# The opening's gated outputs, h and w_down's parts move from pools of their own into the buffers of the later rounds

## The chip, the core and the metric

The kernel runs on one core of a Trainium2 chip. Its engines are TensorE (PE, with weight loads shown apart as PEld), VectorE (DVE), ScalarE (ACT), GpSimd (POOL, hardly used here) and SyncE (SP, which issues nearly all DMAs). Each engine takes the instructions of its own queue strictly in the order in which they stand there, and waits on semaphores for the others. The metric is the device time of one launch in microseconds (us): 1403.15 us is the median of 3 runs before the change (1402.41 to 1403.16).

## The reference

Cut to what matters, with x of 2048 rows by 576 columns, w_gate and w_up of 576 by 4608 and w_down of 4608 by 576:

```python
def _A_ref(x, w_r, w_i):
    X = rfft2(x, axes=(-2, -1)) * (w_r + 1j * w_i)
    return irfft2(X, s=(S, D), axes=(-2, -1))

def _B_ref(x, w_gate, w_up, w_down):
    g = einsum("bsd,df->bsf", x, w_gate)
    u = einsum("bsd,df->bsf", x, w_up)
    return einsum("bsf,fd->bsd", sigmoid(g) * u, w_down)

xn = layernorm(A_x)
out = A_x + _A_ref(xn, A_w_r, A_w_i) + _B_ref(xn, B_w_gate, B_w_up, B_w_down)
```

All of it is float32. The kernel gets float32's accuracy from faster matmuls by splitting each operand into a rounded high part and a low part and adding three products (high by high, high by low, low by high).

## The kernel before

**Tiling.** The 2048 rows are done in two passes of 1024 rows (two chunks of 512, eight tiles of 128). The 4608 inner columns are 36 blocks of 128; each block f in a pass is a "unit" u (u = f in the first pass, 36 + f in the second). Two units make a group j; w_down is applied group by group.

**The opening.** The first group's two units (0 and 1) are done plainly, chunk by chunk, while x is normalised, transposed and split (`opening`, `plain`, `plain_late`). From unit 2 on (`unit`), gate and up projection of both chunks together are a Winograd-like 2 by 2 block product with seven products instead of eight: seven sets of 7 matmuls of 128x512 into the PSUM banks A, B and E (`PRODS`, `prod`, L685). A set that adds into a bank must wait until an earlier sum has been copied out of that bank (ACT, L785, L792 to L803) or added up (DVE, L800, L820). Then y = sigmoid(gate) * up is made on DVE (L822).

**The weights of a unit.** `load_raw` (L254) asks for the raw block of the weights by DMA, two blocks ahead; `make_w` makes the seven factors on DVE (L296 to L299) and splits them into high and low parts on ACT (L272) and DVE (L274, L276); the result is written to DRAM (`wsp`, L303) for the second pass. The buffers of w alternate between two pools: even units use one buffer, odd units the other.

**The down projection.** For the first and last groups `down` multiplies h (the split y) by the split rows of w_down, 12 matmuls of 128x288 for each of the eight row tiles (L853), and DVE adds each product to the accumulator (L862). For the groups between, h and w_down go through seven-product rounds of their own (`seven`, L1081), which take y from the ten places of the tile `ys`, split factors of it into the two buffers `hs` and split factors of w_down into the buffers `wf`; raw w_down lies in `dt` (`load_raw_d`, L931).

**What the change touches.** In the first pass, groups 0 and 1 (units 0 to 3) do not use `ys`, `hs` and `wf`. Unit u < LATE (LATE is 4) writes its gated output into a one-buffer tile `y` (`new_y`), splits it into tiles `h0`, `h1`, `h2` (`new_h`; L723, L724, L829, L830), and the parts of w_down lie in four tiles `wd` (`new_d`, split by `parts_d`, L331 and L333). All of these, with the raw rows `std` and the weights of the odd units, lie in one left-hand pool "a". At the start of unit 4 the pool is closed and `ys`, a pool "m" with w, `hs` and `wf`, and a pool "q" with `qs` are opened over the same addresses; a tile there waits for the last reader of the tiles of "a" that lay below it. On the right-hand side the pool "0" (x's pieces, raw weights) is closed at the same point in favour of a pool "m" with raw weights, the x rows of the later statistics (`xt`, loaded at L380) and `dt`.

**The order of the work.** The program is recorded in the order of the code; a scheduling layer then puts each instruction into its engine's queue by its own estimate of when its inputs and its buffer will be free. So a buffer that comes free later, by that estimate, moves instructions. Some, such as those wrapped in `strictly` and `placed`, keep the order of the code. Each DMA is also given one of eight semaphores in turn and waits for the DMA eight before it.

Of the kernel before, what the change touches and what calls it, by code (L numbers as in the profile page):

```python
# [9 lines left out]
F32 = mybir.dt.float32  # L10
# [153 lines left out]
def spectral_glu_kernel(ctx: ExitStack, tc: tile.TileContext, x, xt, xg, ri, w_in, w_down, out):  # L164
# [57 lines left out]
        L["pool"] = left(lp, f"l{k}")  # L222

    yp, up, U = ExitStack(), ExitStack(), {}

    def upper(k):
        up.close()
        U["pool"] = left(up, f"u{k}")

    lower("a")  # L230

    def split(hi, lo, src, eng=None):
        nc.scalar.activation(hi, src, AF.Copy)
# [9 lines left out]
        return pool  # L243


    WS, RAW, WD, STD = {}, {}, {}, {}

    def load_raw(f, i=None):

# [63 lines left out]
            nc.sync.dma_start(f32(w[:, i]).rearrange("p k m -> p (k m)"), wsp[f][:, i * 5 * P:(i + 1) * 5 * P])  # L313
            yield

    def new_std(j):
        return L["pool"].tile([P, G, D], F32, tag="std", name=f"std{j}", bufs=1)

    def new_d(f):
        return L["pool"].tile([P, 2, D], F32R, tag="wd" + "ab"[f // G], name=f"wd{f}", bufs=G)  # L320

    def load_d(f):
        j, g = divmod(f, G)
        if g == 0 and j:
            STD[j] = new_std(j)
        nc.sync.dma_start(STD[j][:, g], w_down[f])

    def parts_d(f):
        j, g = divmod(f, G)
        st, w = STD[j][:, g], WD[f]  # L330
        placed(nc.scalar.activation(w[:, 0], st, AF.Copy))  # L331
        yield
        nc.vector.tensor_tensor(w[:, 1], st, f32(w[:, 0]), op=OP.subtract)  # L333
        if j not in SEVEN:
            nc.sync.dma_start(wdsp[f], f32(w).rearrange("p a d -> p (a d)"))
        else:
# [324 lines left out]
        yield  # L661


    H, YS, AT = {}, {}, {}
    spare_places = list(range(SLOTS))

    def place(u, c):
# [33 lines left out]

    def new_plain(u, c, begun=None):
# [22 lines left out]

    def of_plain(u, c, b, k):
        return WS[u][:, WP[f"B{k}{b + 1}"]], XA[f"A{c + 1}{k}"]
# [34 lines left out]
    def unit(u, beside):  # L762


        g, v = (hp.tile([P, 2, CW], F32, tag=k, name=f"{k}{u}", bufs=1) for k in ("g", "v"))

        late_h = u >= LATE
        y = None if late_h else new_y(u, 0)

        def one(c):  # L770
            return place(u, c) if late_h else y[:, c]
# [20 lines left out]
        nc.scalar.activation(v[:, 0], bank["B"], AF.Copy)  # L792
# [5 lines left out]
        nc.scalar.activation(v[:, 1], bank["B"], AF.Copy)  # L798
        y1 = one(1)
        nc.vector.tensor_tensor(y1, v[:, 1], bank["E"], op=OP.add)  # L800
        beside(4)
        made(5)
        nc.scalar.activation(g[:, 1], bank["B"], AF.Sigmoid)  # L803
        beside(5)
        if u == LAST - 1:

            nc.vector.tensor_tensor(y1, y1, g[:, 1], op=OP.mult)
            parted(u, 1)
            made(6)
            y0 = one(0)  # L810
            nc.vector.tensor_tensor(y0, v[:, 0], bank["E"], op=OP.add)
            nc.vector.tensor_tensor(y0, y0, g[:, 0], op=OP.mult)
            parted(u, 0)
            beside(6)
            return
        made(6)
        beside(6)

        def first():
            nc.vector.tensor_tensor(one(0), v[:, 0], bank["E"], op=OP.add)  # L820
            h = two(AT[u, 0], AT[u, 1]) if late_h else y
            nc.vector.tensor_tensor(h, h, g, op=OP.mult)  # L822

        ends.append(first)
        if u == NF - 1:
            ends.extend(parting(u, 1) + parting(u, 0))
        if not late_h:
            hh, hl = H[u] if u in H else new_h(u)
            ends.extend([lambda: nc.scalar.activation(hh, y, AF.Copy),  # L829
                         lambda: nc.vector.tensor_tensor(hl, y, f32(hh), op=OP.subtract)])  # L830

    def down(p, j, m, together=True):

# [6 lines left out]
            pd = [ps.tile([P, CW], F32, tag=f"b{b}", name=f"po{j}_{t}_{b}", bufs=1)[:, :HD] for b in "AB"]  # L840
        todo = []
        for g in range(G):
            u = p * NF + j * G + g
            if u not in H:
                h, w = [HS[p, j, c][:, g, i, cols] for i in range(2)], WF[p, j, g].rearrange("p j a d -> p (j a d)").rearrange("p (a d) -> p a d", a=2)
                w = [[w[:, i, b * HD:(b + 1) * HD] for b in range(2)] for i in range(2)]
            else:
                h, w = [v[:, c, cols] for v in H[u]], [[WD[u][:, i, b * HD:(b + 1) * HD] for b in range(2)] for i in range(2)]
# [23 lines left out]

    HS, WF, QS = {}, {}, {}
# [7 lines left out]
    FIRST = set()  # L883

    def new_hs(key, name):
        HS[key] = L["pool"].tile([P, 2, 2, CW], F32R, tag="hs", name=name, bufs=2)
        return HS[key]

    def new_f(key, name):
        WF[key] = L["pool"].tile([P, 2, 2, HD], F32R, tag="wf", name=name, bufs=L["wf"])  # L890
        return WF[key]

    def parting(u, c):

# [16 lines left out]
        for f in parting(u, c):  # L911
            f()

    def flat(w):
        return w.rearrange("p j a d -> p (j a d)").rearrange("p (a d) -> p a d", a=2)
# [5 lines left out]

    def load_raw_d(js, g):

        if not POS:
            DT["d"] = R["pool"].tile([P, G, PLACES, HD], F32, name="dt")
            free_d.extend(range(PLACES))
# [6 lines left out]
    free_d = []  # L933

    def d(js, nm):
        return DT["d"][:, :len(js), POS[js[0], nm]]
# [225 lines left out]
    W = {}  # L1162
    for f in range(G):
        new_w(f)
    STD[0] = new_std(0)
    first_y = new_y(0, 0)
    for f in range(G):
        WD[f] = new_d(f)
    for u in (1, 0, 2):
        new_h(u)  # L1170
    for f in range(G, 2 * G):
        WD[f] = new_d(f)
    for f in range(G):
        w = WS[f]
        for i in (2, 0):
# [231 lines left out]
    def factors():  # L1407
# [54 lines left out]
    for p in range(PAIRS):  # L1462
# [39 lines left out]
        late_input[0] = False  # L1502
        pend = [(p, 0, m) for m in range(0 if p else TPC, TPP)]

        def homes(p):
            L["wf"] = 2 + p
            for tag, shape, n in (("hs", [P, 2, 2, CW], 2), ("wf", [P, 2, 2, HD], 2 + p)):
                L["pool"].tile(shape, F32R, tag=tag, name=f"{tag}_", bufs=n)

        for f in range(G, NF):  # L1510
            u = p * NF + f
            if u == LATE:
                room("m")
                lp.close()
                YS["y"] = left(yp, "yp").tile([P, SLOTS, CW], F32, name="ys")
                lower("m")
                L["pool"].tile([P, NX, 5, P], F32R, tag="w", name="w_", bufs=1)
                homes(0)
                upper("q")
                QS["q"] = U["pool"].tile([P, 3, TPC, HD], F32, name="qs")  # L1520
            if u == NF - 2:
# [89 lines left out]
```

## Time and profile before

| | |
|---|---|
| median of 3 runs | 1403.15 us |
| the profiled execution: its time | 1404.79 us |
| the profiled execution: its span | 1403.0 us |
| PE busy | 1380.9 us (98%) |
| DVE busy | 1046.3 us (75%) |
| ACT busy | 741.6 us (53%) |
| mean granted TensorE clock | 0.996 |
| HBM read and written | 203.99 MB and 131.71 MB |

The span is the profiled execution from its first to its last instruction; the time beside it holds 1.8 us more that lie around it. The units 0 to 3, on which the edit acts, fall into about the first 90 us, and units 4 to 9 into the 100 us behind. In the views below a row of the timeline gives start, length, engine, line and operation with its tiles, and in brackets the idle time ahead of it and what ended it; a row of the windows gives for each engine the busy time and, in brackets, its instructions, then the granted TensorE clock, the DMA engines' busy share and GB/s.

### The profile page before, as it was taken

How to read it: one execution, taken by the hardware profiler on the slowest of the kernel's cores; microseconds unless marked ns; L12 is line 12 of the kernel's file. 1: busy time of each engine (PE TensorE's matmuls, PEld its weight loads, DVE VectorE, ACT ScalarE, POOL GpSimd, SP SyncE). 2: the span in 40 equal slices, each digit the busy share in tenths (PEclk: the TensorE clock that was granted, in tenths of full speed). 3: DMA queues.
4: the chain of work that ended last, by engine and by line, in shares of the span. 5: the costliest groups of instructions: out<-in, count | busy, mean ns of one | idle time of the engine just before them, and what ended most of it. 6: DMA issues, size and time to landing. Idle time of an engine off the chain costs nothing. (4 is left out here: it accounts for less than half of the span.)

```text
span 1403.0 us, 20392 instructions
## 1 busy us (share of the span) xinstructions
PE 1380.9 (98%) x7688; PEld 1206.9 (86%) x7688; DVE 1046.3 (75%) x1521; ACT 741.6 (53%) x1178; POOL 3.3 (0%) x5
## 2 busy tenths in 40 slices
PE   8997999999999999999999999999999999999998
PEld 6885888888888888998888888988888888889888
DVE  7957788888878878899547657666766757676895
ACT  5632666776767776754235545435545434443432
POOL 0000000000000000000000000000000000000000
PEclk9998999999999999999999999999999999999999
DMA  7534677867666677685977777688888688776652
GB/s 253 220 132 194 234 302 291 328 252 298 242 265 260 269 268 276 246 286 179 311 225 220 244 214 219 201 278 271 270 270 266 220 275 255 222 229 190 195 153 85
DMA packets 120657, 337.05 MB, mean 240 GB/s; under 512 B 12560, under 2 KB 29744, under 8 KB 115824
## 3 DMA queue, kind: packets, MB, share of 16 engines
q1 hardware_dynamic: 119568, 334.44, 69.4%
q8 instruction: 61, 1.00, 0.3%
q10 hardware_dynamic: 992, 1.31, 0.3%
q14 instruction: 36, 0.29, 0.1%
HBM read 203.99 MB, written 131.71 MB: 239 GB/s over the span
## 5 line engine op out<-in xcount | busy, mean ns | idle before, releaser
L685 PE MATMUL pB<-X,w 128*128 128x512 f32 x1484 | 381.9, 394 | 2.8 <-ACT v L798 1.1
L1081 PEld LDWEIGHTS ps<-wf,hs 128*128 128x128 f32 x2436 | 348.6, 188 | 20.0 <-DVE acc L1015 0.6
L1081 PE MATMUL ps<-wf,hs 128*128 128x288 f32 x2436 | 361.7, 295 | 0.3 <-DVE hs L1002 0.2
L685 PEld LDWEIGHTS pB<-X,w 128*128 128x128 f32 x1484 | 268.7, 188 | 57.0 <-ACT v L798 4.4
L685 PE MATMUL pE<-X,w 128*128 128x512 f32 x1064 | 275.1, 394 | 0.8 <-ACT w L272 0.6
L685 PE MATMUL pA<-X,w 128*128 128x512 f32 (+1 forms) x1006 | 260.3, 393 | 7.2 <-ACT w L272 5.7
L685 PEld LDWEIGHTS pE<-X,w 128*128 128x128 f32 x1064 | 194.7, 189 | 39.3 <-ACT w L272 1.6
L685 PEld LDWEIGHTS pA<-X,w 128*128 128x128 f32 x1006 | 182.6, 189 | 42.0 <-ACT w L272 6.1
L1002 DVE TENSOR_TENSOR hs<-ys,hs 128x1024 fp32r<-128x1024 f32 (+1 forms) x105 | 124.7, 1188 | 53.5 <-ACT hs L999 52.6
L999 ACT ACTIVATE hs<-ys 128x1024 fp32r<-128x1024 f32 (+1 forms) x105 | 108.0, 1029 | 49.0 <-PE ps L1081 41.7
L272 ACT ACTIVATE w<-raw 128x768 fp32r<-128x768 f32 (+1 forms) x106 | 99.8, 946 | 43.7 <-DVE raw L296 27.4
L274 DVE TENSOR_TENSOR w<-raw,w 128x512 fp32r<-128x512 f32 (+1 forms) x106 | 81.5, 771 | 5.4 <-ACT w L272 3.0
L822 DVE TENSOR_TENSOR ys<-ys,g 128x1024 f32<-128x1024 f32 x65 | 79.5, 1223 | 3.0
L785 ACT ACTIVATE pB<-pA 128x512 f32<-128x512 f32 x68 | 39.6, 583 | 75.0 <-PE pA L685 74.9
L800 DVE TENSOR_TENSOR ys<-v,pE 128x512 f32<-128x512 f32 x66 | 45.2, 684 | 44.6 <-ACT v L798 44.0
L803 ACT ACTIVATE g<-pB 128x512 f32<-128x512 f32 x68 | 40.6, 597 | 66.3 <-PE pB L685 66.2
L995 DVE TENSOR_TENSOR ys<-ys 128x1024 f32<-128x1024 f32 (+1 forms) x60 | 71.1, 1185 | 0.6
L853 PEld LDWEIGHTS po<-wb,hp 128*128 128x128 f32 x468 | 65.1, 188 | 2.6 <-ACT hp L902 0.4
L853 PE MATMUL po<-wb,hp 128*128 128x288 f32 x468 | 67.0, 295 | 0.0
L1015 DVE TENSOR_TENSOR acc<-acc,ps 128x576 f32<-128x576 f32 x55 | 41.4, 752 | 32.4 <-PE ps L1081 32.1
L1015 DVE TENSOR_TENSOR qs<-qs,ps 128x576 f32<-128x576 f32 x62 | 46.6, 751 | 25.1 <-PE ps L1081 25.0
L792 ACT ACTIVATE v<-pB 128x512 f32<-128x512 f32 x68 | 40.5, 595 | 42.6 <-PE pB L685 42.5
(195 smaller groups left out, 1550.1 us busy)
## 6 DMA issues: line engine op xcount, KB each, us to landing
w<-wsp SPq DMA_DIRECT2D x246, 320.0 KB, 3.7
wsp<-w SPq DMA_DIRECT2D x34, 2240.0 KB, 7.2
wf<-fsp SPq DMA_DIRECT2D x105, 288.0 KB, 4.4
fsp<-wf SPq DMA_DIRECT2D x98, 288.0 KB, 3.7
raw<-in_w SPq DMA_DIRECT2D x34, 768.0 KB, 6.8
ri<-in_ri SPq DMA_DIRECT2D x16, 580.0 KB, 5.1
dt<-in_wd SPq DMA_DIRECT2D x32, 288.0 KB, 5.7
xs<-in_xt SPq DMA_DIRECT2D x16, 384.0 KB, 5.7
```

The lines of the kernel that those rows point to most:

```text
L272: placed(nc.scalar.activation(o[:, :, :3, :], src, AF.Copy))
L274: placed(nc.vector.tensor_tensor(o[:, :, 3:, :], src[:, :, :KT, :], f32(o[:, :, :KT, :]), op=OP.subtract))
L685: strictly(nc.tensor.matmul(bank[:, cols], w[:, sw, :], X[:, x, sx, cols], start=start and j == 0, stop=stop and j == len(steps) - 1, skip ...
L800: nc.vector.tensor_tensor(y1, v[:, 1], bank["E"], op=OP.add)
L803: nc.scalar.activation(g[:, 1], bank["B"], AF.Sigmoid)
L822: nc.vector.tensor_tensor(h, h, g, op=OP.mult)
L853: nc.tensor.matmul(pd[b], l, r, start=start, stop=stop)
L995: nc.vector.tensor_tensor(o, at(a), at(b), op=op)
L999: nc.scalar.activation(hs[:, :, 0], o, AF.Copy)
L1002: nc.vector.tensor_tensor(hs[:, :, 1], o, f32(hs[:, :, 0]), op=OP.subtract)
L1015: nc.vector.tensor_tensor(o, a, b, op=op)
L1081: nc.tensor.matmul(pd[:, s], h[:, g, a, m], w[:, g, b], start=q == 0 and not seeded, stop=q == len(parts_) - 1, skip_group_check=seeded)
```

## The change

Units 0 to 3 now use the same tiles as the later ones. `ys` is opened at the very start; so is the pool "m" with w (one buffer), `hs` (two) and `wf` (two in the first pass). Every unit takes its y from a place in `ys` and has it split by `parting` into `hs`, chunk by chunk; the parts of w_down of groups 0 and 1 are `wf` tiles. `std` is alone in an upper pool. With two `hs` buffers for two chunks and two `wf` buffers for two units, group 1's parts are written over group 0's and wait for group 0's products. At unit 4 the left-hand pools stay; only `upper` turns from "a" to "q", and the right-hand pool from "0" to "m", where `dt` is now the first tile. `load_raw_d` for the first round is called at unit 5 (steps 2 and 5) in place of units 4 and 5.

```diff
+    YS = {"y": left(yp, "yp").tile([P, SLOTS, CW], F32, name="ys")}
...
-    lower("a")
+    def homes(p):
+        L["wf"] = 2 + p
+        for tag, shape, n in (("w", [P, NX, 5, P], 1 - p), ("hs", [P, 2, 2, CW], 2), ("wf", [P, 2, 2, HD], 2 + p)):
+            if n:
+                L["pool"].tile(shape, F32R, tag=tag, name=f"{tag}_", bufs=n)
+
+    lower("m")
+    homes(0)
+    upper("a")
...
-    def new_std(j):
-        return L["pool"].tile([P, G, D], F32, tag="std", name=f"std{j}", bufs=1)
-
-    def new_d(f):
-        return L["pool"].tile([P, 2, D], F32R, tag="wd" + "ab"[f // G], name=f"wd{f}", bufs=G)
...
     def load_d(f):
         j, g = divmod(f, G)
-        if g == 0 and j:
-            STD[j] = new_std(j)
+        if g == 0:
+            STD[j] = U["pool"].tile([P, G, D], F32, tag="std", name=f"std{j}", bufs=1)
...
     def parts_d(f):
         j, g = divmod(f, G)
-        st, w = STD[j][:, g], WD[f]
+        st, w = STD[j][:, g], flat(new_f((0, j, g), f"wd{f}"))
...
-    def new_h(u):
-        h = L["pool"].tile([P, 2, 2, CW], F32R, tag=f"h{u % 3}", name=f"h{u}", bufs=1)
-        H[u] = (h[:, 0], h[:, 1])
-        return H[u]
-
-    def new_y(u, c):
-        return L["pool"].tile([P, 2, CW], F32, tag="y", name=f"y{u}_{c}", bufs=1)
...
     def plain_ends(u, c, G_, bank):
-        if u >= LATE:
-            o = place(u, c)
-            ends.append(lambda: nc.vector.tensor_tensor(o, G_, bank[1], op=OP.mult))
-            ends.extend(parting(u, c))
-            return
-        Y = (first_y if (u, c) == (0, 0) else new_y(u, c))[:, 0]
-        hh, hl = (h[:, c] for h in H[u])
-        ends.extend([lambda: nc.vector.tensor_tensor(Y, G_, bank[1], op=OP.mult),
-                     lambda: nc.scalar.activation(hh, Y, AF.Copy),
-                     lambda: nc.vector.tensor_tensor(hl, Y, f32(hh), op=OP.subtract)])
+        ends.append(lambda: nc.vector.tensor_tensor(place(u, c), G_, bank[1], op=OP.mult))
+        ends.extend(parting(u, c))
...
         ends.append(first)
-        if u == NF - 1:
-            ends.extend(parting(u, 1) + parting(u, 0))
-        if not late_h:
-            hh, hl = H[u] if u in H else new_h(u)
-            ends.extend([lambda: nc.scalar.activation(hh, y, AF.Copy),
-                         lambda: nc.vector.tensor_tensor(hl, y, f32(hh), op=OP.subtract)])
+        if u < LATE or u == NF - 1:
+            h, l = zip(*(parting(u, c) for c in ((0, 1) if u < LATE else (1, 0))))
+            ends.extend(lambda fs=fs: [f() for f in fs] for fs in (h, l))
...
-    begin_d = {(LATE, 6): lambda: load_raw_d(js, 0), (LATE + 1, 3): lambda: load_raw_d(js, 1),
+    begin_d = {(LATE + 1, 2): lambda: load_raw_d(js, 0), (LATE + 1, 5): lambda: load_raw_d(js, 1),
...
             if u == LATE:
-                room("m")
-                lp.close()
-                YS["y"] = left(yp, "yp").tile([P, SLOTS, CW], F32, name="ys")
-                lower("m")
-                L["pool"].tile([P, NX, 5, P], F32R, tag="w", name="w_", bufs=1)
-                homes(0)
+                DT["d"] = room("m").tile([P, G, PLACES, HD], F32, name="dt")
                 upper("q")
```

With the buffers the scheduling layer's order changes in the queues of PE, DVE, ACT and SP from about unit 1 to about unit 12; behind that the queues are as they were. Three places follow, before and now. Buffer numbers at the ends of the names are left out or belong to one build; `pA`, `pB`, `pE` are the banks of a unit, `po_0` to `po_7` the eight products of a group's `down`.

**PE, end of unit 4 and start of unit 5, where group 1 is multiplied down.** Before:

```order
L685 MATMUL pB_1029<-X,w_927 128x512 x7
L853 MATMUL po_1_1117<-wd_209,h_208 128x288 x6
L853 MATMUL po_1_1117<-wd_210,h_1004 128x288 x6
L853 MATMUL po_2_1141<-wd_209,h_208 128x288 x6
L853 MATMUL po_2_1141<-wd_210,h_1004 128x288 x6
L853 MATMUL po_3_1172<-wd_209,h_208 128x288 x6
L853 MATMUL po_3_1172<-wd_210,h_1004 128x288 x6
```

and now:

```order
L700 MATMUL pB_1026<-X,w_932 128x512 x7
L839 MATMUL po_1_1116<-wd_872,hp_1_0_915 128x288 x6
L839 MATMUL po_1_1116<-wd_936,hp_1_0_915 128x288 x6
L700 MATMUL pE_1027<-X,w_932 128x512 x7
L839 MATMUL po_2_1137<-wd_872,hp_1_0_915 128x288 x6
L839 MATMUL po_2_1137<-wd_936,hp_1_0_915 128x288 x6
L700 MATMUL pA_1155<-X,w_1040 128x512 x7
L839 MATMUL po_3_1168<-wd_872,hp_1_0_915 128x288 x6
L839 MATMUL po_3_1168<-wd_936,hp_1_0_915 128x288 x6
L700 MATMUL pE_1157<-X,w_1040 128x512 x7
```

Before, the products po_1 to po_7 stood in one run ahead of unit 4's last set (pE) and of the whole of unit 5. Now one product stands between two sets, through to po_7 ahead of unit 5's sixth set.

**DVE, around the addition of po_7, the last product of group 1.** Before:

```order
L862 TENSOR_TENSOR acc<-acc,po_6_1249 128x576
L800 TENSOR_TENSOR ys<-v_1027,pE_1030 128x512
L862 TENSOR_TENSOR acc<-acc,po_7_1275 128x576
L274 TENSOR_TENSOR w_1042<-raw_1005,w_1042 128x3x256
L276 TENSOR_TENSOR w_1042<-raw_1005,w_1042 32x3x128
L820 TENSOR_TENSOR ys<-v_1027,pE_1030 128x512
L296 TENSOR_TENSOR raw_1005<-raw_1005 128x2x384
```

and now:

```order
L793 TENSOR_TENSOR ys<-v_1154,pE_1157 128x512
L848 TENSOR_TENSOR acc<-acc,po_7_1271 128x576
L920 TENSOR_TENSOR wf_2_0_1458<-dt,wf_2_0_1458 128x2x288
L984 TENSOR_TENSOR acc<-acc 128x4x288
L909 TENSOR_TENSOR dt<-dt 128x2x288
L813 TENSOR_TENSOR ys<-v_1154,pE_1157 128x512
L400 BN_STATS st_1592<-xt_1511 128x6
L815 TENSOR_TENSOR ys<-ys,g_1153 128x2x512
L284 TENSOR_TENSOR w_1320<-raw_1303,w_1320 128x3x256
L286 TENSOR_TENSOR w_1320<-raw_1303,w_1320 32x3x128
L920 TENSOR_TENSOR wf_2_1_1504<-dt,wf_2_1_1504 128x2x288
L306 TENSOR_TENSOR raw_1303<-raw_1303 128x2x384
```

Before, unit 5's weights (w_1042) were split behind that addition. Now it is unit 7's weights (w_1320) that stand behind it; those of units 5 and 6 are split ahead of it.

**SP, the requests around unit 5's weights.** Before:

```order
L303 DMA wsp_77<-w_927 128x4480
L380 DMA xt_1046<-in_x 128x576
L303 DMA wsp_78<-w_1042 128x4480
L931 DMA dt<-in_wd 128x576 x2
L254 DMA raw_1155<-in_w 128x1536
```

and now:

```order
L313 DMA wsp_77<-w_932 128x4480
L395 DMA xt_1044<-in_x 128x576
L313 DMA wsp_78<-w_1040 128x4480
L264 DMA raw_1151<-in_w 128x1536
L900 DMA dt<-in_wd 128x576 x4
L264 DMA raw_1303<-in_w 128x1536
```

The request for unit 6's raw weights (raw_1155, raw_1151) still stands behind the store of unit 5's finished weights (wsp_78), now directly. Before, `xt` above it also waited for unit 5's splitting; now it waits for group 1's w_down factors to have left their buffers and for an early transpose.

More of the change, by code (lines that the diff above doesn't have):

```diff
@@ L314, in get_w, with new_hs, new_f, flat @@
             yield
-    def new_std(j):
-        return L["pool"].tile([P, G, D], F32, tag="std", name=f"std{j}", bufs=1)
-    def new_d(f):
-        return L["pool"].tile([P, 2, D], F32R, tag="wd" + "ab"[f // G], name=f"wd{f}", bufs=G)
+    def new_hs(key, name):
+        HS[key] = L["pool"].tile([P, 2, 2, CW], F32R, tag="hs", name=name, bufs=2)
+        return HS[key]
+    def new_f(key, name):
+        WF[key] = L["pool"].tile([P, 2, 2, HD], F32R, tag="wf", name=name, bufs=L["wf"])
+        return WF[key]
+    def flat(w):
+        return w.rearrange("p j a d -> p (j a d)").rearrange("p (a d) -> p a d", a=2)
     def load_d(f):
         j, g = divmod(f, G)
-        if g == 0 and j:
-            STD[j] = new_std(j)
+        if g == 0:
+            STD[j] = U["pool"].tile([P, G, D], F32, tag="std", name=f"std{j}", bufs=1)
         nc.sync.dma_start(STD[j][:, g], w_down[f])
@@ L765, in unit @@
         g, v = (hp.tile([P, 2, CW], F32, tag=k, name=f"{k}{u}", bufs=1) for k in ("g", "v"))
[L767 to L771, printed above, removed]
         bank = {b: ps.tile([P, CW], F32, tag=f"b{b}", name=f"p{b}{u}", bufs=2 if b == "E" else 1) for b in "ABE"}
@@ L798, in unit @@
         nc.scalar.activation(v[:, 1], bank["B"], AF.Copy)
-        y1 = one(1)
+        y1 = place(u, 1)
         nc.vector.tensor_tensor(y1, v[:, 1], bank["E"], op=OP.add)
@@ L809, in unit @@
             made(6)
-            y0 = one(0)
+            y0 = place(u, 0)
             nc.vector.tensor_tensor(y0, v[:, 0], bank["E"], op=OP.add)
@@ L819, in first @@
         def first():
-            nc.vector.tensor_tensor(one(0), v[:, 0], bank["E"], op=OP.add)
-            h = two(AT[u, 0], AT[u, 1]) if late_h else y
+            nc.vector.tensor_tensor(place(u, 0), v[:, 0], bank["E"], op=OP.add)
+            h = two(AT[u, 0], AT[u, 1])
             nc.vector.tensor_tensor(h, h, g, op=OP.mult)
         ends.append(first)
-        if u == NF - 1:
-            ends.extend(parting(u, 1) + parting(u, 0))
-        if not late_h:
-            hh, hl = H[u] if u in H else new_h(u)
-            ends.extend([lambda: nc.scalar.activation(hh, y, AF.Copy),
-                         lambda: nc.vector.tensor_tensor(hl, y, f32(hh), op=OP.subtract)])
+        if u < LATE or u == NF - 1:
+            h, l = zip(*(parting(u, c) for c in ((0, 1) if u < LATE else (1, 0))))
+            ends.extend(lambda fs=fs: [f() for f in fs] for fs in (h, l))
     def down(p, j, m, together=True):
@@ L842, in down @@
         for g in range(G):
[L843 to L848, printed above, removed]
+            h, w = [HS[p, j, c][:, g, i, cols] for i in range(2)], flat(WF[p, j, g])
+            w = [[w[:, i, b * HD:(b + 1) * HD] for b in range(2)] for i in range(2)]
             for n, (i, k) in enumerate(((0, 0), (0, 1), (1, 0))):
@@ L882, in spectral_glu_kernel @@
     DONE = {"S3": "A21", "S4": "A11", "A12": "A12"}
[L883 to L891, printed above, removed]
     def parting(u, c):
@@ L922, in load_raw_d @@
     def load_raw_d(js, g):
-        if not POS:
-            DT["d"] = R["pool"].tile([P, G, PLACES, HD], F32, name="dt")
-            free_d.extend(range(PLACES))
         a, b = free_d.pop(0), free_d.pop(0)
@@ L931, in load_raw_d @@
             nc.sync.dma_start(DT["d"][:, i, a:b + 1:b - a], w_down[G * j + g].rearrange("p (b d) -> p b d", b=2))
-    free_d = []
+    free_d = list(range(PLACES))
     def d(js, nm):
@@ L1164, in spectral_glu_kernel @@
         new_w(f)
[L1165 to L1172, printed above, removed]
     for f in range(G):
@@ L1503, in spectral_glu_kernel @@
         pend = [(p, 0, m) for m in range(0 if p else TPC, TPP)]
[L1505 to L1508, printed above, removed]
         for f in range(G, NF):
```

8 lines of the change are left out of this document (3 added, 5 removed).

## The prediction

> **What bounds the kernel now.** I read the page first: PE is busy for 1380.9 of 1403.0 us, so outside its own work the span holds only some 22 us. Then the windows of the first 180 us, to see where those lie (length, PE, PEld, DVE, ACT, POOL, granted clock, DMA share, GB/s):
>
> ```profile
> 40.00:60.00 20.00, 19.87 (x122) 17.17 (x120) 19.70 (x39) 13.83 (x27) 0.00 (x0) 1.00 0.60 219
> ...
> 80.00:100.00 20.00, 20.00 (x106) 17.22 (x105) 8.22 (x12) 7.97 (x12) 0.00 (x0) 1.00 0.28 116
> 100.00:110.00 10.00, 10.00 (x69) 9.51 (x69) 6.30 (x10) 0.00 (x0) 0.00 (x0) 1.00 0.00 0
> 110.00:120.00 10.00, 7.89 (x31) 5.19 (x30) 7.00 (x10) 3.26 (x5) 0.00 (x0) 1.00 0.19 60
> 120.00:130.00 10.00, 4.21 (x18) 2.80 (x16) 5.09 (x8) 2.48 (x4) 0.00 (x0) 0.97 1.00 397
> 130.00:140.00 10.00, 8.77 (x20) 6.16 (x21) 9.22 (x15) 3.70 (x5) 0.00 (x0) 0.52 0.49 197
> ...
> 160.00:180.00 20.00, 19.64 (x99) 16.08 (x98) 19.62 (x28) 16.14 (x24) 0.00 (x0) 1.00 0.42 173
> ```
>
> There is one hole, from 110 to 140 us: PE idles, then its clock falls to 0.52. Ahead of it, from 80 to 110, ACT and the DMAs are mostly idle and DVE is about half idle: work that could have been done then was not. The waits say what PE and SP stood for (us in total, times, longest):
>
> ```profile
> PE pA L685 <- ACT w L272: 5.7, 1, 5.7
> ...
> SPq L380 <- DVE w L276: 34.0, 1, 34.0
> ```
>
> The timeline of that stretch gives the chain:
>
> ```profile
> 96.36 11.35 PE L853 MATMUL po<-wd,h 128*128 128x288 f32 x84
> ...
> 97.06 1.16 ACT L272 ACTIVATE w<-raw 128x1152 fp32r<-128x1152 f32 x1
> ...
> 106.82 0.68 DVE L800 TENSOR_TENSOR ys<-v,pE 128x512 f32<-128x512 f32 x1
> 107.55 1.46 PEld L685 LDWEIGHTS pE<-X,w 128*128 128x128 f32 x7
> 107.55 1.88 PE L685 MATMUL pE<-X,w 128*128 128x512 f32 x7
> ...
> 108.42 0.95 DVE L274 TENSOR_TENSOR w<-raw,w 128x768 fp32r<-128x768 f32 x1
> ...
> 116.68 0.41 DVE L276 TENSOR_TENSOR w<-raw,w 32x256 fp32r<-32x256 f32 x1
> ...
> 117.23 0.33 SPq L380 DMA_DIRECT2D xt<-in_x  x1
> ...
> 119.79 1.22 SPq L254 DMA_DIRECT2D raw<-in_w  x1
> ...
> 123.14 1.76 PE L685 MATMUL pE<-X,w 128*128 128x512 f32 x7
> ...
> 129.40 1.16 ACT L272 ACTIVATE w<-raw 128x1152 fp32r<-128x1152 f32 x1 [1.22 <-DMA raw<-in_w]
> ...
> 130.62 3.49 PE L685 MATMUL pA<-X,w 128*128 128x512 f32 x7 [5.72 <-ACT w L272]
> ...
> 142.27 1.88 PE L685 MATMUL pB<-X,w 128*128 128x512 f32 x7 [0.23 <-ACT v L792]
> ```
>
> Seven of group 1's products run in one block (84 matmuls in 11.35 us). DVE adds them one by one and reaches unit 5's weights only at 108.42, though their first high part was there at 98.2. They are done at 117.1, in pieces that PE waits for; only then does SP get past `xt`, and the raw weights of unit 6 are asked for at 119.79. They are there 9.6 us later, and PE starts unit 6 at 130.62, at half clock. So the hole is not a lack of any engine's time. It is the order of the queues.
>
> **What the hole costs.** The rate that PE keeps without waits:
>
> ```profile
> 150.46 1.75 PE L685 MATMUL pB<-X,w 128*128 128x512 f32 x7
> 152.04 1.75 PE L685 MATMUL pA<-X,w 128*128 128x512 f32 x7
> ```
>
> that is 1.58 us from set to set. From the row at 107.55 to the row at 142.27 are 34.72 us. PE's queue has 84 matmuls of 128x512 there, twelve sets of seven: 12 x 1.58 = 19.0. **Lost: 15.7 us.** By the same rows 4.5 of it lie before 123.14 (15.59 for seven sets, 11.1), 5.9 in the gap (7.48 for one set), 5.3 behind it (11.65 for four sets, 6.3), where the clock is low and DVE makes the next weights just in time.
>
> The Trainium skill (TensorE: Matmul & The Clock Gate, section What's actually happening) has PE's clock halve after an idle window of about 3.4 us and return after a busy one. The 0.52 behind the 5.9 us gap agrees. By that rule a stall well under 3.4 us draws no slow clock behind it, so the small new stalls below would cost their own length only; were each to halve the clock for one window, an estimate from the page's figure is 1.7 us more for each.
>
> **What the change removes.** The products of group 1 read `hs` and `wf`, which no new tile overlays at unit 4, and in the new order one of them stands between two sets. Unit 5's weights are split ahead of unit 4's last set. I follow unit 6's raw weights, the transfer that was late. They are asked for when unit 5's weights are done, which in DVE's queue is ahead of the sum that unit 4's last set waits for; so at least one set and one product before unit 5 starts, 1.6 + 1.6 = 3.2 us (84 in 11.35 gives 1.6 for a product of 12). Unit 5 now takes seven sets and five products, 11.1 + 8.1 = 19.2. From request to need there are thus 22 us, against 9.6 of transfer (119.79 to 129.40, behind a store of the same size as now) and 2.1 for the first split (1.16 + 0.95). About 10 us are to spare, and the hole should go: **-15.7**.
>
> **What it adds.** Three waits, each costed from both sides. The durations come from the groups by shape in 40 to 300 us:
>
> ```profile
> L274 DVE TENSOR_TENSOR w<-raw,w 128x512 fp32r<-128x512 f32 x30 | 20.5, 684 | 0.1
> L274 DVE TENSOR_TENSOR w<-raw,w 128x768 fp32r<-128x768 f32 x16 | 15.3, 954 | 3.9 <-DMA fsp<-wf 2.2 <-ACT w L272 1.6
> L822 DVE TENSOR_TENSOR ys<-ys,g 128x1024 f32<-128x1024 f32 x12 | 14.7, 1222 | 0.5
> L296 DVE TENSOR_TENSOR raw<-raw 128x768 f32<-128x768 f32 x15 | 14.3, 953 | 0.1
> L276 DVE TENSOR_TENSOR w<-raw,w 32x256 fp32r<-32x256 f32 x30 | 12.5, 415 | 0.7
> L951 DVE TENSOR_TENSOR wf<-dt,wf 128x576 fp32r<-128x576 f32 x16 | 12.1, 754 | 2.0 <-ACT wf L948 1.9
> L276 DVE TENSOR_TENSOR w<-raw,w 32x384 fp32r<-32x384 f32 x16 | 8.8, 547 | 0.3
> L298 DVE TENSOR_TENSOR raw<-raw 128x384 f32<-128x384 f32 x15 | 8.3, 553 | 0.1
> L800 DVE TENSOR_TENSOR ys<-v,pE 128x512 f32<-128x512 f32 x12 | 8.2, 681 | 4.8 <-ACT v L798 4.7
> L385 DVE BATCH_NORM_STATS2 st<-xt 128x6 f32<-128x288 f32 x14 | 6.0, 452 | 3.3 <-DMA xt<-in_x 3.3
> L1015 DVE TENSOR_TENSOR acc<-acc 128x1152 f32<-128x1152 f32 x1 | 1.4, 1360 | 0.0
> ...
> L272 ACT ACTIVATE w<-raw 128x768 fp32r<-128x768 f32 x30 | 25.1, 841 | 11.8 <-DVE raw L296 11.0 <-DVE raw L299 0.8
> ```
>
> *Group 1's parts wait for group 0's.* The split of w_down for unit 2 on ACT now waits for po_7 of group 0. Behind it on ACT stand three more operations and then the copy of unit 3's bank B, which PE wants 20 matmuls of 128x512 later (6 in E, 7 in B, 7 in A), 20 x 0.226 = 4.5 us. Four operations at up to 0.84 (L272, the longest of them) are 3.4 us. Cover is left, but little; if it is gone, one copy is late by a microsecond. 0 to 1: **+0.3**.
>
> *The order in 40 to 66 us.* DVE is full there (19.70 of 20). Four of x's sums now stand ahead of a split that PE's transposes wait for, each 0.45 long:
>
> ```profile
> 56.26 0.95 DVE L296 TENSOR_TENSOR raw<-raw 128x768 f32<-128x768 f32 x1
> 57.12 0.45 DVE L449 TENSOR_TENSOR xa<-xa 128x288 f32<-128x288 f32 x1
> ```
>
> That is up to +1.8; against it, two splits of w_down (0.75 each) leave this stretch for the one behind po_7, up to -1.5. The bounds nearly cancel: **+0.3**. The second fence row also starts 0.09 before the first ends, so DVE's operations overlap a little when they do not depend on each other.
>
> *Units 6 and 7 have no products between their sets.* What the hole put off and the run of products hid is now due here. Between the sum that releases unit 5's last set and the one that releases unit 6's, DVE's queue holds one addition and one `dt` sum (both of 576 columns like the 0.754 of L951), two splits to `wf` (0.754 each), the sum of two accumulators (1.360), three sums for ys (2 x 0.681 + 1.222), two statistics (0.452 each) and a unit's weights (0.954 + 0.547 + 0.953 + 2 x 0.553 + 2 x (0.684 + 0.415)): 13.6 us, or 12.0 if each of some 20 overlaps by 0.08. PE has 53 matmuls there, 12.0 us. So a stall of 0 to 1.6 in unit 6: **+1.0**. For unit 7 the same count (two statistics, three sums for ys, a unit's weights, and one split to `hs`, as wide as L822) gives 10.5 of DVE against 50 matmuls or 11.3 of PE, but ACT's copies of bank B stand behind splits that wait for DVE: 0 to 1.6, **+0.5**. From unit 8 on rounds stand between the sets again; before, in 160 to 180 us, DVE worked at 19.62 of 20 and PE still at 19.64, so I take nothing there.
>
> The number of matmuls and the bytes are as before. Sum: -15.7 + 0.3 + 0.3 + 1.0 + 0.5 = **-13.6 us**. The profiled execution's span goes from 1403.0 to 1389.4 (its time was 1404.79, 1.8 more, and lies 1.6 above the median). On the median of 1403.15 the same difference gives **1389.6 us**. With all costs at their low ends (-15.7 - 1.5) it would be 1386.0, with all at their high ends (+1 + 1.8 + 1.6 + 1.6) 1393.5.
>
> **The rivals.**
> *DVE stays behind* (chance 0.14). The splits of units 5 to 8 wait for each other without slack, and each of the four pays unit 6's high end: 4 x 1.6 = 6.4 in place of 1.5, and the early two costs 0.6 as above: 1403.15 - 15.7 + 0.6 + 6.4 = 1394.5. For it: 19.62 of 20 in 160 to 180. Against: from 80 to 120 DVE is busy for only four to seven tenths, and the new order works there.
> *The hole moves to a later unit* (0.04). If unit 7's weights are late once as unit 6's were, a gap and its slow clock come back, 5.9 + 5.3 = 11.2: 1403.15 - 13.6 + 11.2 = 1400.8, no change that shows. Against it stand the 10 us to spare.
> *SP's queue stops twice* (0.04), the slower side. Each request for `xt` now waits for DVE's statistics of the `xt` before it and stands ahead of a raw request; before, one such wait held SP for 34 us. If the statistics are reached more than 10 us after their place in the plan, raw weights of units 8 and 10 come late, each with 11.2: 1403.15 - 13.6 + 22.4 = 1412. Against it: the statistics stand early in DVE's queue, next to sums that PE waits for.
>
> **How the numbers follow.** The forecast, 1388 to 1392, has 0.68; a better end, with hardly any new stall, 0.10; the rivals 0.14, 0.04 and 0.04. A measurement of this kernel tells about 0.2% (2.8 us) from no change. Forecast, better end and the first rival are faster by more: 0.92. The hole that moves is "same", 0.04; SP's stop is slower, 0.04. The range for 8 in 10 reaches from the low ends, 1386.5, to the first rival, 1395.
>
> **What would show it.** In the changed kernel's profile: no window of 10 us between 100 and 150 us with a clock under 0.9; the longest wait of PE behind 40 us under 2 us; the 34.0 us wait of SP at the `xt` load gone; the po matmuls of group 1 in pieces of 12; unit 6's raw weights asked for before unit 5 starts; DVE over 9 in ten in units 5 and 6 (about 105 to 135 us), where the new stalls would lie. I am wrong if PE waits for split weights (ACT or DVE w) by more than 3 us in one piece, or if a copy of bank B (v) or a sum for ys becomes PE's steady wait in units 5 to 9.

## The result, and the profile after

The changed kernel takes 1386.57 us (median of 4 runs, 1386.0 to 1386.7), the kernel before 1403.16 (4 runs, 1402.41 to 1404.3): a ratio of 0.988, 95% interval 0.9863 to 0.9897. That is 16.6 us less where 13.6 were forecast. Of the profiled executions, span against span, the gain is larger: 1384.1 against 1403.0, 18.9 us, since the profiled execution of before (1404.79) was one of its longer ones.

The windows of the changed kernel, with the columns as before (length, PE, PEld, DVE, ACT, POOL, granted clock, DMA share, GB/s):

```profile
40.00:60.00 20.00, 19.74 (x126) 17.34 (x125) 19.33 (x38) 12.32 (x26) 0.00 (x0) 1.00 0.51 186
80.00:100.00 20.00, 20.00 (x104) 17.08 (x103) 15.14 (x26) 8.64 (x14) 0.00 (x0) 1.00 0.68 260
100.00:110.00 10.00, 10.00 (x62) 9.06 (x61) 5.42 (x8) 2.35 (x3) 0.00 (x0) 1.00 0.91 333
110.00:120.00 10.00, 10.00 (x55) 8.79 (x54) 9.91 (x16) 4.65 (x7) 0.00 (x0) 1.00 0.43 177
120.00:130.00 10.00, 9.92 (x44) 7.88 (x43) 9.87 (x18) 5.02 (x8) 0.00 (x0) 1.00 0.84 280
130.00:140.00 10.00, 9.98 (x44) 7.92 (x43) 8.59 (x14) 6.33 (x9) 0.00 (x0) 1.00 0.89 338
160.00:180.00 20.00, 19.97 (x109) 17.40 (x108) 15.60 (x21) 12.53 (x19) 0.00 (x0) 1.00 0.94 346
```

The hole is gone: PE stands idle for 0.10 us between 100 and 140, where it stood for 9.13 before, and the clock is 1.00 throughout. From 80 to 100 DVE works for 15.14 in place of 8.22, and the DMAs move 260 GB/s in place of 116: the work that came late is done there. The window from 160 to 180, where DVE was full (19.62), now holds later work. The work that stood there before lies at about 142 to 162 now: there DVE is busy for 18.49 of 20 us and PE for all 20.

The timeline of the changed kernel has the chain, link by link:

```profile
85.37 1.17 ACT L282 ACTIVATE w<-raw 128x1152 fp32r<-128x1152 f32 x1 [0.99 <-PE pE L700]
...
94.43 0.32 SPq L313 DMA_DIRECT2D wsp<-w  x1
94.80 0.42 SPq L264 DMA_DIRECT2D raw<-in_w  x1
...
101.78 1.75 PE L839 MATMUL po<-wd,hp 128*128 128x288 f32 x12
...
104.36 1.17 ACT L282 ACTIVATE w<-raw 128x1152 fp32r<-128x1152 f32 x1 [1.74 <-DMA raw<-in_w]
...
119.33 1.75 PE L700 MATMUL pA<-X,w 128*128 128x512 f32 x7
...
127.26 1.07 PE L700 MATMUL pA<-X,w 128*128 128x512 f32 x4
```

Unit 5's first split is at 85.37 (before: 97.06), its finished weights are stored at 94.43, and unit 6's raw weights are asked for at 94.80, 25 us earlier than before (119.79). They are there at 104.36, again 9.6 us later, and PE starts unit 6 at 119.33. Group 1's products stand one by one (x12). The longest wait of PE behind the start, and SP's for DVE at `xt`:

```profile
PE pa L542 <- ACT qs L1032: 0.6, 1, 0.6
```
```profile
SPq L395 <- DVE mv L401: 1.2, 2, 0.8
```

How the lead grew can be read from ACT's copy of bank A into bank B, which comes once per unit (L785 before, L778 now). Before:

```profile
87.08 0.58 ACT L785 ACTIVATE pB<-pA 128x512 f32<-128x512 f32 x1 [1.73 <-PE pA L685]
...
248.51 0.59 ACT L785 ACTIVATE pB<-pA 128x512 f32<-128x512 f32 x1
```

and now:

```profile
86.44 0.58 ACT L778 ACTIVATE pB<-pA 128x512 f32<-128x512 f32 x1
...
229.17 0.59 ACT L778 ACTIVATE pB<-pA 128x512 f32<-128x512 f32 x1
```

| copy of unit | before | now | lead |
|---|---|---|---|
| 4 | 87.08 | 86.44 | 0.64 |
| 6 | 134.57 | 121.18 | 13.39 |
| 7 | 149.13 | 133.03 | 16.10 |
| 10 | 197.13 | 177.93 | 19.20 |
| 13 | 248.51 | 229.17 | 19.34 |
| 68 | 1345.93 | 1327.05 | 18.88 |

All of it is made between units 4 and 10 (copies of neighbouring units can stand a set apart in the two orders, so a single step of the table is rough); behind that the lead stays. At unit 4 the copy understates PE's lead, since ACT now splits unit 5's weights (85.37) ahead of it: the last three matmuls of unit 4's first set, with the same number of matmuls ahead of them in both kernels, start at 86.14 before and 85.17 now, a lead of 0.97. Most of that is not the edit's: at the first matmuls of 128x512, where both programs are still alike, the lead is 0.79 (16.16 against 15.37), because the fifteen identity matmuls at the start took 6.58 and 5.62 us.

### The profile page after: what moved, and what is told of

Its sections match the earlier page's. It is cut to its first block, busy times and chain, and to the rows that moved or that the text cites. A ratio compares the mean times of both kernels' runs of the same rounds, so it can differ in the third digit from the quotient of the medians.

```text
span 1384.1 us, 20414 instructions
## 1 busy us (share of the span) xinstructions
PE 1371.5 (99%) x7688; PEld 1204.6 (87%) x7688; DVE 1046.0 (76%) x1523; ACT 742.0 (54%) x1180; POOL 3.3 (0%) x5
## 5 line engine op out<-in xcount | busy, mean ns | idle before, releaser
L700 PE MATMUL pE<-X,w 128*128 128x512 f32 x1064 | 271.8, 392 | 0.0
L700 PE MATMUL pA<-X,w 128*128 128x512 f32 (+1 forms) x1006 | 256.4, 390 | 0.5 <-ACT X L476 0.2
L700 PEld LDWEIGHTS pA<-X,w 128*128 128x128 f32 x1006 | 181.7, 188 | 34.1 <-ACT g L788 1.1
L793 DVE TENSOR_TENSOR ys<-v,pE 128x512 f32<-128x512 f32 x68 | 46.5, 684 | 44.0 <-ACT v L791 43.2
L778 ACT ACTIVATE pB<-pA 128x512 f32<-128x512 f32 x68 | 39.6, 583 | 64.5 <-PE pA L700 64.4
L813 DVE TENSOR_TENSOR ys<-v,pE 128x512 f32<-128x512 f32 x67 | 45.8, 683 | 22.7 <-PE pE L700 22.1
```

The costliest lines, as they stand in the source:

```text
L700: strictly(nc.tensor.matmul(bank[:, cols], w[:, sw, :], X[:, x, sx, cols], start=start and j == 0, stop=stop and j == len(steps) - 1, skip ...
L813: nc.vector.tensor_tensor(place(u, 0), v[:, 0], bank["E"], op=OP.add)
```

## The experiments

**The right-hand half alone.** `dt` as the first tile of the right-hand pool, and its first loads in unit 5:

```diff
...
-    begin_d = {(LATE, 6): lambda: load_raw_d(js, 0), (LATE + 1, 3): lambda: load_raw_d(js, 1),
+    begin_d = {(LATE + 1, 2): lambda: load_raw_d(js, 0), (LATE + 1, 5): lambda: load_raw_d(js, 1),
...
-                room("m")
+                DT["d"] = room("m").tile([P, G, PLACES, HD], F32, name="dt")
```

> The kernel before with the right-hand half of the change alone: dt is the first tile of the right-hand pool and the first round's raw w_down is asked for in unit 5; y, h, the w_down parts and the odd units' weights still lie in the pool that is closed at unit 4. Theory: the hole comes from the left-hand overlay, where ys waits for the readers of h and wd, so that group 1's products run in one block and DVE reaches unit 5's weights behind them. This half leaves that as it is: about 1403 us (1401 to 1404.5), a gap of PE at unit 6 of 4 to 7 us, half clock behind it. Rival: it is the transfers (dt's loads among the raw weights, SP standing at xt) that made unit 6 late; then 1388 to 1394 us and no gap over 2 us.

Measured: 1401.82 us (11 runs, 1399.74 to 1403.04) beside 1403.6 of before (27 runs, 1401.58 to 1406.55), ratio 0.9982 [0.9973, 0.9991]. Its wait, SP's requests and two windows:

```profile
PE pA L685 <- ACT w L272: 3.4, 1, 3.4
```
```profile
116.86 0.32 SPq L303 DMA_DIRECT2D wsp<-w  x1
117.27 0.39 SPq L254 DMA_DIRECT2D raw<-in_w  x1
117.76 4.71 SPq L928 DMA_DIRECT2D dt<-in_wd  x4
```
```profile
120.00:130.00 10.00, 5.92 (x20) 3.88 (x19) 4.57 (x6) 3.04 (x4) 0.00 (x0) 0.89 0.97 359
130.00:140.00 10.00, 9.22 (x37) 6.56 (x36) 9.88 (x17) 5.66 (x8) 0.00 (x0) 0.94 0.42 175
```

The hole stays, as the first theory has it, but is shorter than it said: with no load of `dt` ahead of it, the request for unit 6's raw weights is at 117.27 instead of 119.79, and the gap is 3.4 instead of 5.7 us. The half clock behind it is shorter too, but this profile is of the shortest of the eleven executions (mean clock 0.999, the others 0.996 to 0.998), so that part can't be laid to the edit. The loads of `dt` cost 2.3 us of the gap, and 1.8 us in the medians; the rest is the left-hand half's.

**The left-hand half alone.** The changed kernel with those lines as before:

```diff
+        if not POS:
+            DT["d"] = R["pool"].tile([P, G, PLACES, HD], F32, name="dt")
...
-    begin_d = {(LATE + 1, 2): lambda: load_raw_d(js, 0), (LATE + 1, 5): lambda: load_raw_d(js, 1),
+    begin_d = {(LATE, 6): lambda: load_raw_d(js, 0), (LATE + 1, 3): lambda: load_raw_d(js, 1),
...
-                DT["d"] = room("m").tile([P, G, PLACES, HD], F32, name="dt")
+                room("m")
```

> The changed kernel with its right-hand half undone: ys, hs, wf and the odd units' weights have their homes from the start, but dt is made late and the first round's raw w_down is asked for in units 4 and 5 again, two of its loads ahead of unit 6's raw weights. Theory: the left-hand half carries the whole gain; the two loads ahead of the raw weights cost a part of the 10 us to spare and no time: 1386.0 to 1388.5 us, no wait of PE over 1 us behind 40 us. Rival: the order of the transfers counts; unit 6's raw weights come late, a gap of 2 to 6 us and half clock behind it: 1393 to 1400 us.

Measured: 1386.64 us (4 runs, 1386.51 to 1387.4), ratio 0.9877 [0.9864, 0.9891], the whole gain. SP in its timeline:

```profile
95.15 0.34 SPq L395 DMA_DIRECT2D xt<-in_x  x1
95.54 0.42 SPq L313 DMA_DIRECT2D wsp<-w  x1
96.06 1.61 SPq L902 DMA_DIRECT2D dt<-in_wd  x2
97.72 1.24 SPq L264 DMA_DIRECT2D raw<-in_w  x1
```

`xt` waits for unit 5's splits again (12.3 us at the queue) and two loads of `dt` stand ahead of the raw weights, but the splits are early, the request is at 97.72, and no wait of PE behind 40 us is over 0.6 us. With DVE early, these entries ahead of the request in SP's queue cost nothing that shows.

**The raw weights' request moved up, in the kernel before.**

```diff
             if u == LATE:
...
+                load_raw(u + 2)
...
-            if u + 2 < NF:
+            if u + 2 < NF and u != LATE:
                 load_raw(u + 2)
```

> The kernel before, with the request for unit 6's raw weights moved up from the end of unit 4 to its start, so that it stands ahead of the xt load and of the store of unit 5's weights in SP's queue; all else is as before, group 1's block of 84 matmuls too. Theory: of the 15.7 us lost in the hole, 4.5 lie before unit 5's late sets (DVE's order) and stay, while the 5.9 of the gap and most of the 5.3 at half clock go: 1391.5 to 1395 us. Rival: DVE, late with unit 5's weights, is late with unit 6's as well, even with the raw weights there; the gap shrinks by 2 to 3 us only, 1398 to 1401 us.

Measured: 1403.37 us (11 runs, 1402.63 to 1403.6), ratio 0.9995 [0.9986, 1.0004]. Neither theory gave that. Its queue of SP, the timeline and a window:

```profile
SPq L254 <- DVE w L276: 34.1, 1, 34.1
```
```profile
117.15 0.33 SPq L254 DMA_DIRECT2D raw<-in_w  x1
...
124.61 0.61 PE L685 MATMUL pA<-X,w 128*128 128x512 f32 x2
...
133.25 1.39 SPq L254 DMA_DIRECT2D raw<-in_w  x2
...
143.61 1.15 ACT L272 ACTIVATE w<-raw 128x1152 fp32r<-128x1152 f32 x1
...
143.76 4.03 PE L1081 MATMUL ps<-wf,hs 128*128 128x288 f32 x14 [3.20 <-ACT hs L999]
```
```profile
140.00:150.00 10.00, 6.80 (x25) 5.83 (x24) 6.07 (x7) 4.26 (x5) 0.00 (x0) 0.66 0.84 302
```

The request itself now waited 34.1 us for unit 5's splits: the new right-hand pool's raw buffer is free only when unit 5's raw weights have been read. So it went out at 117.15, only 2.6 us earlier. With no store and no other load just ahead of it the weights were also there sooner, 5.9 us after the request (split from 123.06) in place of 9.6. Together that was enough to start unit 6 at 124.61 instead of 130.62. But unit 7's raw weights are asked for at 133.25, when unit 6's splits are done, and split from 143.61; meanwhile PE has only a round's products to go on with, stands for 3.2 us until their `hs` is split from unit 6's y, and then runs at half clock. Unit 7's own first set starts at 147.59. The copy of unit 6 leads before by 7.18 us, that of unit 7 lags by 1.77. **The hole moved one unit on and cost the same.** Here the late start of the weights couldn't be mended at one request: unit 6 handed its lateness to unit 7.

**The first `xt` two units later, in the kernel before.**

```diff
-            if p == 0 and f and f % 4 == 0:
+            if p == 0 and (f == 6 or f > 4 and f % 4 == 0):
```

> The kernel before, with the first later statistics (the xt load at which SP stood for 34.0 us) two units later. Theory: xt is not what makes unit 6's raw weights late, since the store of unit 5's weights, next in SP's queue, waits for the same splits on DVE: 1402 to 1404 us, the same gap. Rival: SP's stand at xt is the cause; without it the raw weights come 10 us or more earlier: 1390 to 1396 us.

Measured: 1402.21 us (11 runs, 1401.22 to 1404.51), ratio 0.9991 [0.9982, 1.0]. Its waits:

```profile
PE pA L685 <- ACT w L272: 4.9, 1, 4.9
```
```profile
SPq L303 <- DVE w L276: 125.3, 13, 34.0
```

As the theory had it: the 34.0 us pass from `xt` to the store behind it, and the gap stays.

**Group 1's products in one block again, in the changed kernel.**

```diff
             spots = {i: 1 for i in (range(5) if f % G else range(4, 7))}
+            if u == LATE:
+                spots = {5: 1, 6: 7}
+            elif u == LATE + 1:
+                spots = {}
```

> The changed kernel with group 1's products put back into one block near the end of unit 4 (one at step 5, seven at step 6, none in unit 5); unit 5's weights are still split ahead of them and unit 6's raw weights still asked for early. First theory: of the 4.5 us lost ahead of 123.14 before, most was not DVE's order but that unit 5 had no product between its sets while ACT copied a bank (PE waits of 0.73, 0.69 and 0.69 with about 0.25 each to fill up again); these come back with the block and nothing else does: 1388.5 to 1391 us, three waits of about 0.7 in unit 5, no gap over 2 us, no half clock. Second: the block by itself makes the hole, since DVE's additions bunch with it: a gap over 3 us and 1396 us or more. Third: with the weights there early, sets of the next unit fill the waits: 1386.5 to 1387.5 us.

Measured: 1387.26 us (4 runs, 1386.82 to 1387.89), ratio 0.988 [0.9867, 0.9894] beside 1404.6 of before on this chip: the changed kernel's ratio. Its timeline:

```profile
98.82 11.35 PE L839 MATMUL po<-wd,hp 128*128 128x288 f32 x84
110.00 1.77 PE L700 MATMUL pA<-X,w 128*128 128x512 f32 x7
...
117.96 1.07 PE L700 MATMUL pA<-X,w 128*128 128x512 f32 x4
118.87 1.84 PE L700 MATMUL pB<-X,w 128*128 128x512 f32 x7
```

The third theory holds. The block of 84 matmuls in 11.35 us by itself does no harm that shows. With unit 6's weights there in time, four of its first matmuls stand between two of unit 5's bank B sets (117.96), so that PE has work while ACT copies the bank. In the kernel before, unit 5's waits were:

```profile
111.75 1.21 PE L685 MATMUL pA<-X,w 128*128 128x512 f32 x4 [0.73 <-ACT pB L785]
...
115.54 0.73 PE L685 MATMUL pB<-X,w 128*128 128x512 f32 x2 [0.26 <-ACT w L272]
116.70 1.45 PE L685 MATMUL pB<-X,w 128*128 128x512 f32 x5 [0.43 <-DVE w L274]
118.83 1.89 PE L685 MATMUL pB<-X,w 128*128 128x512 f32 x7 [0.69 <-ACT v L792]
121.41 1.89 PE L685 MATMUL pB<-X,w 128*128 128x512 f32 x7 [0.69 <-ACT v L798]
```

Three of the five are copies of a bank that PE stood through with nothing else to multiply.

**More work for DVE, in the changed kernel.**

```diff
                 QS["q"] = U["pool"].tile([P, 3, TPC, HD], F32, name="qs")
+                nc.gpsimd.memset(QS["q"][:, 0], 0.0)
...
                 if (u, i) in begin_d:
                     begin_d[u, i]()
+                if LATE + 1 < u < LATE + 4 and i in (1, 3, 5):
+                    q = QS["q"][:, 0, :2]
+                    tc.keep_in_program_order(nc.vector.tensor_tensor(q, q, q, op=OP.subtract))
```

> The changed kernel with six more subtractions of 128x576 on DVE (a corner of qs, which is not in use there, is zeroed and then subtracted from itself), three in the splitting of unit 7's weights and three in that of unit 8's: 6 x 0.754 = 4.5 us of DVE, about 4.0 with the overlap of 0.08 each. First theory: DVE has next to nothing to spare behind unit 6, as the forecast's +1.0 and +0.5 took it; most of it lands on PE: 1389 to 1391 us. Second: the small stalls seen there (0.5 us in all) mean that DVE has slack; from 130 to 160 us it is idle for some 3 of 30 us, so a good half is hidden: 1387 to 1388.5 us. Third: all is hidden, 1386.5 to 1387 us.

Measured: 1387.35 us (4 runs, 1387.09 to 1387.62), ratio 0.9881 [0.9866, 0.9896]. Two of its windows:

```profile
120.00:130.00 10.00, 9.59 (x43) 7.61 (x41) 9.89 (x16) 5.49 (x8) 0.00 (x0) 1.00 0.68 224
130.00:140.00 10.00, 10.00 (x43) 7.76 (x44) 9.04 (x14) 5.25 (x7) 0.00 (x0) 1.00 0.85 303
```

DVE is a little fuller, and PE's idle time from 120 to 140 is 0.41 instead of 0.10 us. From unit 4's copy to unit 13's it takes 143.51 us against the changed kernel's 142.73: 0.8 of the added 4.0 us reach PE. The second theory, at its low end: DVE at 9.9 of 10 in one window has slack in the next.

**The left-hand pool closed and opened again at unit 4, in the changed kernel.** The same tiles at the same addresses:

```diff
                 DT["d"] = room("m").tile([P, G, PLACES, HD], F32, name="dt")
+                up.close()
+                lower("m")
+                homes(0)
                 upper("q")
```

> The changed kernel with one thing put back: at unit 4 the left-hand pool with w, hs and wf is closed and opened again, with the same tiles at the same addresses; ys stays as it is. No tile of unit 5 then lies over anything that group 1's products read, other than its own next use. First theory: what set the order before is the closing of the pool itself, since the scheduling layer takes every tile of the new pool as free only when the last reader in the old one is through; unit 5's weights are then placed behind all of group 1's products, and the hole comes back: 1398 to 1404 us, a gap over 3 us at unit 6. Second: only tiles that lie over one another count; then the order and the time stay as in the changed kernel, 1386.5 to 1387.5 us.

Measured: 1403.84 us (11 runs, 1401.23 to 1406.03), ratio 0.9996 [0.9987, 1.0005] beside 1404.6. Its timeline and waits:

```profile
99.34 9.74 PE L839 MATMUL po<-wd,hp 128*128 128x288 f32 x72
...
111.19 0.95 DVE L284 TENSOR_TENSOR w<-raw,w 128x768 fp32r<-128x768 f32 x1
...
112.19 1.43 PE L700 MATMUL pA<-X,w 128*128 128x512 f32 x5 [2.64 <-DVE w L284]
...
117.82 1.90 SPq L264 DMA_DIRECT2D raw<-in_w  x1
```
```profile
PE pA L700 <- DVE w L284: 3.2, 2, 2.6
PE pA L700 <- ACT w L282: 1.7, 1, 1.7
PE pE L700 <- ACT w L282: 1.7, 1, 1.7
```
```profile
110.00:120.00 10.00, 7.08 (x23) 5.39 (x24) 8.01 (x13) 2.06 (x3) 0.00 (x0) 0.83 0.21 84
```

The whole gain is lost with three lines. The products stand in one run of 72 matmuls, unit 5's weights are split on DVE from 111.19, behind the last addition, and the raw weights of unit 6 are asked for at 117.82. No tile of unit 5 lies over what group 1's products read, so no overlay of one tile on another is needed: **the closing of the pool is enough.** The order reads as if the scheduling layer took the writers of the new pool's tiles to wait for the last readers in the old one (its estimates are not in the profile); on the chip, ACT's first split of unit 5 (96.84) didn't wait for them. The losses lie in several short waits here, the longest 2.64, in place of one of 5.7, and the medians come out the same. The profile is of the shortest of the eleven executions, 1401.23 us.

## Why the prediction was wrong, point by point

*What bounds the kernel, and that the hole goes (-15.7): right.* The links were late splits on DVE, a late request, a late transfer, an idle PE, a slow clock; with unit 5's splits early all of them are gone. In two of its reasons it was inexact. It put the order down to tiles that overlay what group 1's products read; the reopened pool shows that the closing alone is enough (the kernel before has both). And of the 4.5 us ahead of 123.14 it said that PE waits for unit 5's pieces; of those waits' 2.8 us three quarters (0.73 + 0.69 + 0.69) are bank copies, which PE stands through because the next unit's weights are not there to be multiplied meanwhile; with them there, in the bunched kernel, these waits are gone.

*"The order in 40 to 66 us" and "group 1's parts wait for group 0's", +0.3 each: too high by about 0.8.* PE's lead goes from 0.79 at the first matmuls of 128x512 to 0.97 at unit 4, so both together cost nothing, and 0.2 was won.

*Units 6 and 7, +1.0 and +0.5: too high by about one.* This is the smaller of the two mis-sized steps behind the hole. By the rate of 1.58 per set, PE's rows from 106.56 to 134 lose 0.5 us in all: 0.24 and 0.15 around the set at 128.41, the rest less. The count of DVE's work against PE's was made unit by unit, as if what DVE has over in one unit were lost for the next. With the weights a unit ahead it is not: even 4.0 us more on DVE cost 0.8.

*"From unit 8 on ... I take nothing there": wrong by about three.* This is the larger one. From the starts in unit 4 (86.14 before, 85.17 now) to those by unit 13's copy (247.84 and 228.48) both kernels do the same work, 444 matmuls of 128x512 and 312 of 128x288. Before, it took 161.70 us and now it takes 143.31: 18.4 less. The hole's 15.7 is in it. From 142.27 to there the kernel before loses another 4.0 us against the rate of these matmuls (0.227 and 0.132 us from start to start), most of it in some twenty waits and slower matmuls behind them, 0.1 to 0.4 each. The changed kernel loses 0.8 from 134 on, so 3.2 came off where the prediction took nothing.

The prediction read PE's 19.64 of 20 beside a full DVE (19.62) as harmless. But a busy PE is not PE at its rate: in that row 60 matmuls of 128x512 and 37 of 128x288 start, 18.5 us at the rate above, so that one window loses about 1.5. In the changed kernel 60 and 48 start from 142 to 162, and nothing is lost. DVE has a part in it: of the waits of PE's weight loads between 142 and 260 the profile puts 2.5 of 4.2 us down to DVE, and in the changed kernel, from 134 to 241, 0.2 of 1.3. That the backlog behind the hole makes these small losses is argued from this, not shown: no run took it away alone, and DVE is nearly as full (18.49 of 20) in the changed kernel's stretch without a loss.

*From the profile to the median.* By span, -18.9 = -0.8 (the start) - 0.2 (up to unit 4) - 15.7 + 0.5 (units 6 and 7) - 3.2, and 0.5 given back in small pieces behind unit 13. On the medians 16.6 remain, since the profiled execution of before was 1.6 above its median and that of the changed kernel 0.6 below. The prediction set the hole's 15.7, read from that longer execution, against the median as it was. Times of the kernel before go with the mean clock: of the 27 executions beside the first four experiments (1401.58 to 1406.55), 14 at 0.996 have a median of 1404.6, 11 at 0.997 one of 1402.5. So the hole was probably cheaper in the median execution, which hid a part of the miss. The changed kernel, without a slow stretch in the middle, spreads over 0.7 in its four.

*The rivals.* DVE did not stay behind. The hole that moves to a later unit didn't occur in this change, but is what the kernel with the early request does. SP didn't stop twice; `xt` now waits for DVE for 0.8 us at the longest.

*What was to show it:* no clock below 1.00 between 100 and 150; the longest wait of PE behind 40 us was 0.6; the wait of 34.0 us gone; po in pieces of 12; the raw weights asked for at 94.80, ahead of unit 5; DVE at 9.9 in ten from 110 to 130. All as written but the last, for DVE is at 5.4 in ten from 100 to 110 and at 8.6 from 130 to 140; and where it was full, that was no sign of a stall.

## What to carry to other kernels

Where a scheduling layer places instructions by when a buffer is free, closing a pool in mid-stream can hold back the tiles of the next pool, also those that lie on nothing that is still read; pools that stay open through the change of stage keep the queue's order. Look for the work that could have been done earlier (a half idle engine ahead of a hole) rather than for the transfer at whose end the wait is booked: a request moved up alone only moved the hole. And size what a backlog costs up to the unit where the kernel is level again, not only to the end of the visible gap, and by the number of matmuls that start, not by the busy share.

## What the runs showed of the hardware

The half clock behind a gap comes in lengths that are not set by the gap alone. From the windows, twice the missing share of the clock times the window gives 10.2 us in the kernel before (0.97 and 0.52), 10.2 with the late `xt` (0.89 and 0.60), 6.8 with the early request (0.66), 3.4 with the right-hand half (0.89 and 0.94) and 3.4 in the reopened pool (0.83): one, two or three times 3.4. The longest waits of PE were 5.7, 4.9, 3.2, 3.4 and 2.6 us. The changes lie on a grid: in the kernel before the clock changes at 9.89, 129.36, 139.60 and 1402.53 us, whole multiples of 3.413 us apart.

The multiples of 3.4 agree with the free-running window of about 3.4 us that the Trainium skill (TensorE: Matmul & The Clock Gate, section What's actually happening) gives. Cut into windows on that grid, the profiles also show when the clock changed (shares of a window in which PE was busy):

| kernel | last window ahead of the drop | windows at half clock, in order |
|---|---|---|
| before | 0 | 0.63, 0.82, 1.00 |
| late `xt` | 0.36 | 0.22, 0.82, 1.00 |
| early request | 0.33 | 0.74, 1.00 |
| right-hand half | 0.08 | 0.93 |
| reopened pool | 0.49 | 1.00 |

The Trainium skill has the clock halve after an idle window, and the prediction took from it that a stall well under 3.4 us does no more than its own length. Here the window need not be idle throughout: in the reopened pool one wait of 2.64 us with one of 0.73 behind it was enough. That one busy window brings the clock back, as the Trainium skill has it too, agrees with all five: the clock returned at the end of the first window in which PE was busy for 0.93 or more, and waits inside the windows (0.82 and less) made it two or three. Where the limits lie was not tried: windows of 0.51 and 0.52 in the reopened pool drew no drop, and neither did one of 0.46 at the end of the kernel with the left-hand half alone.
